# An FFT filter, a soft mixture of experts and a gated MLP in one kernel: the order of the copies in a software-pipelined loop, and the steps in which its side work is issued

## The chip, the cores and the metric

One core of one Trainium2 chip. The metric is the device time in microseconds, median of the runs; the kernel before took 1748.12 us (three runs, 1746.44 to 1748.21).

## The reference

Eight sequences of 3072 tokens and 256 channels (`x`) go through three layers, all in float32:

1. a frequency filter: `X = rfft(x)` along the sequence, a complex 256 x 256 product with `w_r + i w_i` and a bias, a soft threshold of 0.01 on the real and imaginary part, and `irfft`;
2. a soft mixture of experts over all 24576 tokens and 32 slots: `logits = x @ phi`, a softmax over the tokens (`d`) that mixes tokens into slots, eight small two-layer experts on four slots each, and a softmax over the slots (`c`) that spreads the slots back to tokens;
3. a gated MLP: RMS norm, `silu(xn @ w_gate) * (xn @ w_val)`, times `w_out`; its weights come as 64-bit floats.

```python
X = rfft(x); Y = soft(X.real @ w_r - X.imag @ w_i + b_r) + 1j * soft(X.real @ w_i + X.imag @ w_r + b_i)
x = irfft(Y).reshape(-1, 256)
logits = x @ phi;  d = softmax(logits, axis=0);  slot_in = d.T @ x
c = softmax(logits, axis=1);  x = c @ experts(slot_in)
xn = x / rms(x) * rms_g;  out = (silu(xn @ w_gate) * (xn @ w_val)) @ w_out
```

## The kernel before

Two phases. **Phase 2** (from about 655 us on) is the gated MLP; the change leaves it alone. **Phase 1** takes the eight sequences ("batches" below) through the filter and gathers the slots. The result of the filter is never transformed back for all tokens; logits and slot sums are formed from the frequencies.

Phase 1 is one loop of 288 **steps**: 36 per batch, in three windows of 12 (`w`, `m = u % 12`). Each step issues for TensorE, in this order: a part of **M** (the complex product, `emit_M`, one or three matmuls, in the two `psM` banks), then where they fall on the step: `emit_0`, **A** (first stage of the transform of the next batch, eight groups a batch, `emit_A`, in `psC`), **T** (turning the filtered frequencies, `emit_T`, in `psT` or `psA`), **L** (products with `phi`, `emit_L`, same banks), **B** (second stage of the next window, `emit_B`, in two `psB` banks), and last the parts of the **slots' chain** of the batch before that belong to TensorE. All engines work their queues in program order.

Work that follows a matmul is not issued with it but put off with `post(f, k, rank)`: `f` is issued `k` steps later, at the start of that step, sorted by `rank`; after it come the chain's parts for the other engines, then the matmuls. What is put off:

- A: `asb`, a copy of `psC` to SBUF on ScalarE (L246), then two stores to a `bounce` buffer in DRAM (SyncE's queue), one step later, rank 1; the load of the input for the group three later is put off too (rank 1, ahead of it).
- B: two copies on ScalarE one step later (L282, L283), a sum and a difference on VectorE two steps later (L286, L287), rank 0.
- M: for each `psM` bank either a copy on ScalarE (L322), or `whole`, a sum on VectorE that frees the bank (L329), then `first` on ScalarE (L332) and `end` on VectorE (L335), which completes the filtered frequencies; all rank 0.
- T: a copy on ScalarE (L383); L: a turn on VectorE (L396); both one step later, rank 1.

`psC` is a single tile of two banks, used in turn by A and by the parts of the chain. `load_B` brings the bounced data of the next batch back (four transfers on SyncE's queue, L260); its first quarter for a new batch is issued at step 23, and TensorE needs it at step 27.

**The chain** (`chain(b)`, a list of step, function and a mark for TensorE's parts): `binv`, `t1`, `ainv` (logits by token, two matmuls into `psC`, each copied by ScalarE, L437), `dmax` (L448, the largest logit of each slot over the batch), `dpar` (a reduction across partitions on GpSimd, L453, `PARTITION_ALL_REDUCE`), `dmn`, `dsub` (VectorE), `dexp` (ScalarE); beside it `cmax`, `csub` (GpSimd, L497), `cexp`, `csum`, `cmul` (GpSimd, L511) and a store of `c` to DRAM (L513, SyncE); then `fa`, `t2` (VectorE, L528), `fb`, `dT`, `slot`, `s_up`.

**The converter** (`converter`, 18 pieces) makes float32 of the MLP's weights: a load (L128), six to eight VectorE operations (L144 to L155), a product on GpSimd (L156) and a store (L165); the last six pieces also a ScalarE copy (L160) and a difference on GpSimd (L162). It is a generator; the loop takes its next step (to the next `yield`) when a running sum `load` of VectorE work, kept from the hand-written tables `fixed` and `chained` and the number `pace`, is under `room`.

Ahead of the loop the first batch's eight A groups run straight through: 16 loads on SyncE's queue, then two stores to `bounce` a group, with the loads of `bf`, `wf` and `w_i` behind the fifth group's stores, then `load_B(0, 0)`, on which TensorE's first B waits.

Of the kernel before, what the change touches and what calls it, by code (L numbers as in the profile page):

```python
# [6 lines left out]
F32 = mybir.dt.float32  # L7
# [3 lines left out]
ALU = mybir.AluOpType  # L11
# [98 lines left out]
def converter(tc, st, w_gate, w_val, w_out, wgv_d, wo_d):  # L110

    nc = tc.nc
    raw_p, tmp_p = pool(tc, st, "cvr", 2), pool(tc, st, "cv", 1)
    jobs = []
    for i, w in enumerate((w_gate, w_val)):
        v = w.bitcast(I32).rearrange("(k p) f -> p k f", p=128)
        for k in range(2):
            for f in range(3):
                jobs.append((v[:, k, 1024 * f:1024 * f + 1024], wgv_d[:, k, 1536 * i + 512 * f:1536 * i + 512 * f + 512]))
    v = w_out.bitcast(I32).rearrange("(k p) c -> p k c", p=128)  # L120
    for k in range(0, 12, 2):
        jobs.append((v[:, k:k + 2, :], tuple(w[:, k:k + 2, :].rearrange("p k c -> p (k c)") for w in wo_d)))

    def load(n):
        t = raw_p.tile([128, 512, 2], I32, name="cvraw")
        v = jobs[n][0]
        d = t.rearrange("p n w -> p (n w)")
        nc.sync.dma_start(out=d if len(v.shape) == 2 else d.rearrange("p (k f) -> p k f", k=2), in_=v)  # L128
        return t

    def steps():
        v = nc.vector
        nxt = load(0)
        yield
        for n, (_, dst) in enumerate(jobs):
            t = nxt
            if n + 1 < len(jobs):
                nxt = load(n + 1)
            lo, hi = t[:, :, 0], t[:, :, 1]
            p = tmp_p.tile([128, 512], I32, name="cva")  # L140
            m = tmp_p.tile([128, 512], I32, name="cve")
            q = tmp_p.tile([128, 512], I32, name="cvr")

            v.tensor_scalar(out=p, in0=hi, scalar1=0x7FF00000, scalar2=None, op0=ALU.bitwise_and)  # L144
            v.tensor_scalar(out=p, in0=p, scalar1=float(896 << 20), scalar2=float(1151 << 20), op0=ALU.max, op1=ALU.min)
            yield
            v.tensor_scalar(out=p, in0=p, scalar1=float(896 << 20), scalar2=8.0, op0=ALU.subtract, op1=ALU.mult)
            v.scalar_tensor_tensor(out=p, in0=hi, scalar=-(1 << 31), in1=p, op0=ALU.bitwise_and, op1=ALU.bitwise_or)
            yield
            v.tensor_scalar(out=m, in0=hi, scalar1=3, scalar2=0x7FFFFF, op0=ALU.logical_shift_left, op1=ALU.bitwise_and)  # L150
            v.tensor_scalar(out=m, in0=m, scalar1=0x3F800000, scalar2=None, op0=ALU.bitwise_or)
            yield
            v.tensor_scalar(out=q, in0=lo, scalar1=8, scalar2=0xFFFFFF, op0=ALU.logical_shift_right, op1=ALU.bitwise_and)
            w = m.bitcast(F32)
            v.scalar_tensor_tensor(out=w, in0=q, scalar=2.0 ** -44, in1=w, op0=ALU.mult, op1=ALU.add)  # L155
            nc.gpsimd.tensor_tensor(out=w, in0=w, in1=p.bitcast(F32), op=ALU.mult)  # L156
            if isinstance(dst, tuple):
                h = q.bitcast(F32)
                yield
                nc.scalar.activation(out=h.bitcast(F32R), in_=w, func=AF.Copy)  # L160
                nc.sync.dma_start(out=dst[0], in_=h)
                nc.gpsimd.tensor_tensor(out=w, in0=w, in1=h, op=ALU.subtract)  # L162
                nc.sync.dma_start(out=dst[1], in_=w)
            else:
                nc.sync.dma_start(out=dst, in_=w)  # L165
            yield
    return steps()


def phase1(tc, x, w_r, w_i, b_r, b_i, phi, t_d, t_bf, t_ci, t_ai, t_af, t_id,  # L170
# [56 lines left out]
    def emit_A(g, banks=None):  # L227
# [16 lines left out]
        def evac():  # L244
# [6 lines left out]
            for h in range(2):  # L251
                f = 512 * (2 * i + h)
                nc.sync.dma_start(out=v[:, :, f:f + 512], in_=Y[64 * h:64 * h + 48].rearrange("k (o f) -> k o f", o=2))
        post(evac)

    def load_B(b, q):
        t = bin_p.tile([128, 4, 256], F32, name="bin")
# [39 lines left out]
    def emit_M(b, qq, m):  # L297
# [36 lines left out]
        def end():  # L334
            nc.vector.scalar_tensor_tensor(out=Y, in0=Y, scalar=b_hi[:, ri, ch:ch + 1], in1=r[:, o:], op0=ALU.add, op1=ALU.min)  # L335
            if m == 11:
                xq.pop((b, qq))
                xs.pop((b, qq))
        post(whole, 1 + late, 0)
        post(first, 2 + late, 0)  # L340
        post(end, 3 + late, 0)

# [30 lines left out]
    def emit_T(b, q, ri, ps=None):  # L373
        Y = yy[b, q // 2]
        if (b, q) not in yts:
            yts[b, q] = new_yt(b, q)
        ps = new_t() if ps is None else ps
        for par in range(2):
            for h in range(2):
                o = 256 * par + 128 * h  # L380
                nc.tensor.transpose(out=ps[:, o:o + 128], in_=ysl(Y, slice(q % 2, q % 2 + 1), h, ri, par), identity=ident)
        yt = yts[b, q]
        post(lambda: nc.scalar.activation(out=yt[:, 2 * ri:2 * ri + 2, :].rearrange("p a c -> p (a c)"), in_=ps, func=AF.Copy))  # L383

    def emit_L(b, qq):
        Y = yy[b, qq]
# [6 lines left out]
                nc.tensor.matmul(out=ps[32 * g:32 * g + 32, 0:256], lhsT=ph[:, h, :],  # L393
                                 rhs=ysl(Y, slice(0, 2), h, ri, par), start=(h == 0), stop=(h == 1))
        lf = lfs[b]
        post(lambda: nc.vector.transpose(out=lf[:, 8 * qq:8 * qq + 8, :].rearrange("p a s -> p (a s)"), in_=ps[:, 0:256]))  # L396

    def bank(p, n):
        return p.tile([128, 512], F32, name=n)
# [4 lines left out]
    def chain(b):  # L404
# [20 lines left out]
        def ainv(k, own=None):  # L425
            if k == 0:
                S["l"] = ch_p.tile([128, 1024], F32, name="ch")[0:96]
            s = slice(512 * k, 512 * k + 512)
            if own:
                ps = S["l", 16 * k] = bank(*own)[0:96]  # L430
            else:
                if k == 0:
                    S["ps"] = new_c()
                ps = S["ps"][0:96, s]
            nc.tensor.matmul(out=ps, lhsT=ai, rhs=S["t1"][:, s], start=True, stop=True)
            if not own:
                post(lambda: nc.scalar.activation(out=S["l"][:, s], in_=ps, func=AF.Copy))  # L437

        def lcopy(k):
            nc.scalar.activation(out=S["l"][:, 512 * k:512 * k + 512], in_=S["l", 16 * k], func=AF.Copy)  # L440
# [65 lines left out]
            nc.vector.tensor_scalar(out=sc, in0=sc, scalar1=1e-9, scalar2=None, op0=ALU.add)  # L506
            nc.vector.reciprocal(out=sc, in_=sc)

        def cmul():
            S["c"] = ch_p.tile([128, 1024], F32, name="ch")[0:96]  # L510
            nc.gpsimd.tensor_tensor(out=S["c"].rearrange("p (n s) -> p n s", s=32), in0=S["e"].rearrange("p (n s) -> p n s", s=32),  # L511
                                    in1=S["sc"].unsqueeze(2).to_broadcast([96, 32, 32]), op=ALU.mult)
            nc.sync.dma_start(out=c_d[b], in_=S["c"])  # L513

# [9 lines left out]
        def t2(s0, s1):  # L524
            if s0 == 0:
                S["t2"] = ch_p.tile([128, 1024], F32, name="ch")
            ps = S["ps"][:, 32 * s0:32 * s1] if s1 - s0 == 32 else S["ps", s0]
            nc.vector.transpose(out=S["t2"].rearrange("p (a s) -> p s a", s=32)[:, s0:s1],  # L528
                                in_=ps.rearrange("p (s n) -> p s n", n=32))

# [63 lines left out]
            return lambda: f(*a)  # L594

        if b < NB - 1:
            return [(5, clear), (6, L(binv, 0, 24), 1), (7, L(t1, 0, 32)), (8, L(ainv, 0), 1), (9, L(ainv, 1), 1),
                    (12, L(dmax, 0, 32)), (13, L(dpar, 32)), (14, cmax), (15, csub), (18, L(dmn, 32)), (18, L(dsub, 0, 32)),
                    (19, L(dexp, 0, 32)), (19, alexp), (20, cexp), (21, csum), (22, cmul), (22, L(fa, 0, 16), 1),
                    (23, L(fa, 16, 32), 1), (24, L(t2, 0, 32)), (25, alT),  # L600
                    (26, L(fb, 0, 12), 1), (27, L(fb, 12, 24), 1), (29, L(dT, 0, 6)),
                    (31, lambda: slot(0, 6, new_c()), 1), (33, s_up)]

        def tr(q, ri, k):
            return lambda: emit_T(b, q, ri, bank(*((psT, "psT"), (psM, "psM"), (psM, "psM"), (psA, "psA"), (psB, "psB"))[k]))
# [47 lines left out]
    banks = [(psA, "psA"), (psT, "psT"), (psB, "psB"), (psB, "psB"), (psM, "psM"), (psM, "psM")]  # L653
    for g in range(8):
        emit_A(g, [bank(*banks[2 * (g % 3) + o]) for o in range(2)])
        if g == 4:
            load_bf(0, nc.sync)
            for t, w in ((wf, w_r), (rw[:, 0:512].rearrange("p (k m) -> p k m", k=2), w_i)):
                nc.sync.dma_start(out=t, in_=w.rearrange("(k p) m -> p k m", p=128))
    warm_up(14)  # L660
    prep_w()
    load_B(0, 0)
# [7 lines left out]
    for c in range(-6, 0):  # L670
# [9 lines left out]
            emit_A(8)  # L680
        elif c == -2:
            emit_B(0, 1, 1)
    first = [1, 4, 6, 9, 11, 14, 17] + [36 * b + u for b in range(NB - 2) for u in (34, 36, 38, 47, 49, 51, 53, 55)]
    first = {u: 9 + g for g, u in enumerate(first)}


# [4 lines left out]


    fixed = (1.8, 0.75, 0.75, 0.0, 0.0, 1.55, 0.7, 1.1, 1.45, 0.0, 1.85, 0.7)
    chained = {5: 0.3, 7: 1.1, 12: 1.8, 14: 1.2, 18: 1.5, 21: 1.6, 24: 2.0, 29: 1.0, 30: 2.0, 33: 0.5, 34: 2.0}
    load, room, pace = 0.0, 1.0, 1.72
    for u in range(S):
        w, m = divmod(u, 12)
        b, qq = divmod(w, 3)
# [492 lines left out]
```

## Time and profile before

| | |
|---|---|
| median of three runs | 1748.12 us |
| the profiled execution, whole | 1743.32 us |
| its span, first to last instruction | 1741.5 us |
| TensorE busy | 1679.0 us (96%) |
| VectorE busy | 1289.5 us (74%) |
| ScalarE busy | 1026.0 us (59%) |
| GpSimd busy | 106.6 us (6%) |
| mean granted TensorE clock | 0.993 |

The page is one execution. TensorE is busy nearly throughout, so the time is its work plus the time in which it waits; the rows that matter are those that tell what it waited for, and in which stage. A matmul's end is modelled, so its busy time runs a little past the start of the next.

### The profile page before, as it was taken

What the parts mean: (1) busy time and instruction counts of PE and PEld (TensorE: products, weight loads), DVE (VectorE), ACT (ScalarE), POOL (GpSimd) and SP (SyncE); (2) the same over time, 40 slices, a digit from 0 to 9 for tenths busy, and PEclk for the clock granted to TensorE, in tenths of its full rate; (3) what the DMA queues carried; (4) which work ended last, traced back from release to release, by engine and by line L of the source; (5) the groups of instructions that cost most, each with busy time, mean ns of one, the idle gap of its engine ahead of it and who ended that gap; (6) DMA issues with size and microseconds to landing.
All of it is one profiled execution on the core that took longest, in us unless ns stands there. A gap on an engine that the chain in (4) does not pass through costs nothing.

```text
span 1741.5 us, 27023 instructions
## 1 busy us (share of the span) xinstructions
PE 1679.0 (96%) x10173; PEld 1289.7 (74%) x10173; DVE 1289.5 (74%) x2257; ACT 1026.0 (59%) x1942; POOL 106.6 (6%) x74
## 2 busy tenths in 40 slices
PE   6999998989999899999999999999999999999999
PEld 3565554645556547888888888888888888888887
DVE  3577776676665758877877887887887887787775
ACT  2555545445554437666666666666666666666664
POOL 0001201020220101000000000000000000000000
PEclk8999999999999999999999999999999999999999
DMA  9875665556556483020021021021021020020001
GB/s 245 253 211 158 201 159 165 148 157 186 136 152 203 141 262 99 25 63 29 17 61 34 25 61 34 25 61 34 25 61 34 25 60 25 22 60 26 25 25 37
DMA packets 111138, 164.20 MB, mean 94 GB/s; under 512 B 15376, under 2 KB 76528, under 8 KB 111008
## 3 DMA queue, kind: packets, MB, share of 16 engines
q1 hardware_dynamic: 107456, 161.66, 32.0%
q8 instruction: 80, 1.31, 0.3%
q10 hardware_dynamic: 3376, 0.62, 0.2%
q0 software_dynamic: 176, 0.20, 0.1%
q14 instruction: 50, 0.41, 0.1%
HBM read 90.08 MB, written 59.77 MB: 86 GB/s over the span
## 4 chain that ended last, share of the span: by engine, by line
PE 83%; DVE 6%; ACT 5%; DMA 4%; issue 1%; SPq 1%; POOL 0%; ACTq 0%; DVEq 0%; POOLq 0%
PE po L1092 15%; PE pe L1092 15%; PE po L1093 8%; PE pe L1093 8%; PE pg L1064 8%; PE pv L1066 8%; PE psM L316 5%; PE psB L273 4%; PE psC L240 3%; PE psM L311 2%; ACT asb L246 1%; DMA bounce<-asb 1%; PE psC L576 1%; DVE yy L329 1%; DVE yy L335 1%
## 5 line engine op out<-in xcount | busy, mean ns | idle before, releaser
L1070 DVE TENSOR_TENSOR h<-s,pv 128x512 f32<-128x512 f32 x576 | 395.2, 686 | 189.2 <-ACT s L1068 180.5
L1068 ACT ACTIVATE s<-pg 128x512 f32<-128x512 f32 x576 | 344.7, 599 | 300.4 <-PE pg L1064 298.9
L1092 PE MATMUL po<-wo,hh 128*128 128x512 f32 x1152 | 429.2, 396 | 0.0
L1092 PE MATMUL pe<-wo,hh 128*128 128x512 f32 x1152 | 425.6, 394 | 0.0
L107 DVE TENSOR_TENSOR hl<-h,hh 128x512 fp32r<-128x512 f32 x572 | 400.4, 700 | 0.1
L106 ACT ACTIVATE hh<-h 128x512 fp32r<-128x512 f32 x576 | 359.7, 625 | 1.0 <-DVE h L1070 0.9
L1093 PE MATMUL po<-wo,hl 128*128 128x256 f32 x1152 | 323.9, 281 | 0.0
L1093 PE MATMUL pe<-wo,hl 128*128 128x256 f32 x1152 | 322.8, 280 | 0.0
L1092 PEld LDWEIGHTS po<-wo,hh 128*128 128x128 f32 x1152 | 216.8, 188 | 50.9
L1092 PEld LDWEIGHTS pe<-wo,hh 128*128 128x128 f32 x1152 | 216.5, 188 | 49.4
L1093 PEld LDWEIGHTS pe<-wo,hl 128*128 128x128 f32 x1152 | 216.5, 188 | 22.7
L1064 PE MATMUL pg<-cq,gst 128*128 128x512 f32 x576 | 228.7, 397 | 0.3 <-ACT s L1068 0.3
L1066 PE MATMUL pv<-cq,gst 128*128 128x512 f32 x576 | 226.3, 393 | 1.0 <-DVE h L1070 1.0
L1093 PEld LDWEIGHTS po<-wo,hl 128*128 128x128 f32 x1152 | 216.2, 188 | 2.7
L316 PE MATMUL psM<-xq,wh 128*128 128x512 f32 x384 | 165.8, 450 | 6.0 <-DVE yy L329 5.2
L282 ACT ACTIVATE xq<-psB 128x512 fp32r<-128x512 f32 x96 | 57.2, 596 | 144.0 <-PE psB L273 143.8
L1064 PEld LDWEIGHTS pg<-cq,gst 128*128 128x128 f32 x576 | 108.4, 188 | 26.8 <-ACT s L1068 1.1
L332 ACT ACTIVATE r<-yy,b_lo 128x512 f32<-128x512 f32 (+1 forms) x92 | 66.9, 727 | 92.4 <-DVE yy L329 46.6
L273 PEld LDWEIGHTS psB<-bf,bin 128*128 128x128 f32 x768 | 98.1, 197 | 30.6 <-issue 27.2
L273 PE MATMUL psB<-bf,bin 128*128 128x128 f32 x768 | 105.3, 282 | 15.1 <-DMA bin<-bounce 15.1
L286 DVE TENSOR_TENSOR xs<-psB,xs 128x256 f32<-128x256 f32 x96 | 40.5, 421 | 102.6 <-ACT xs L283 102.6
L1066 PEld LDWEIGHTS pv<-cq,gst 128*128 128x128 f32 x576 | 108.8, 189 | 2.3 <-DVE h L1070 2.2
(229 smaller groups left out, 1762.1 us busy)
## 6 DMA issues: line engine op xcount, KB each, us to landing
bin<-bounce SPq DMA_DIRECT2D x192, 128.0 KB, 3.8
out_dram<-o SPq DMA_DIRECT2D x47, 512.0 KB, 2.9
xraw<-in_x_dram SPq DMA_DIRECT2D x112, 192.0 KB, 4.0
bounce<-asb SPq DMA_DIRECT2D x112, 192.0 KB, 3.6
ex<-in_moe_w_dram SPq DMA_DIRECT2D x16, 1024.0 KB, 9.5
cq<-chi SPq DMA_DIRECT2D x56, 96.0 KB, 2.1
cq<-clo SPq DMA_DIRECT2D x56, 96.0 KB, 2.1
yt<-in_x_dram SPq DMA_DIRECT2D x16, 192.0 KB, 6.1
```

The source lines that it names most:

```text
L106: nc.scalar.activation(out=hi, in_=src, func=AF.Copy)
L107: (lo_eng or nc.vector).tensor_tensor(out=lo, in0=src, in1=hi.bitcast(F32), op=ALU.subtract)
L273: nc.tensor.matmul(out=ps[:, 128 * j:128 * j + 128], lhsT=t[:, j, 128 * h:128 * h + 128], rhs=bf[:, 4 * q + j, :], start=True, stop=True)
L282: nc.scalar.activation(out=hi, in_=v, func=AF.Copy)
L316: nc.tensor.matmul(out=ps, lhsT=w[k - 1][:, h, cs], rhs=X[:, p, h, k - 1], start=(h == 0 and n == 0), stop=(h == 1 and n == 2))
L332: nc.scalar.activation(out=r[:, o:], in_=Y, func=AF.Relu, bias=b_lo[:, ri, ch:ch + 1])
L1064: nc.tensor.matmul(out=pg, lhsT=gst[:, 128 * fb:128 * fb + 128], rhs=v, start=True, stop=True)
L1066: nc.tensor.matmul(out=pv, lhsT=gst[:, 1536 + 128 * fb:1536 + 128 * fb + 128], rhs=v, start=True, stop=True)
L1068: nc.scalar.activation(out=s, in_=pg, func=AF.Silu)
L1070: nc.vector.tensor_tensor(out=h, in0=s, in1=pv, op=ALU.mult)
L1092: nc.tensor.matmul(out=ps, lhsT=hh[:, ts], rhs=wo[:, fb].rearrange("p k c -> p (k c)"), start=(fb == 0), stop=False)
L1093: nc.tensor.matmul(out=ps[:, 0:256], lhsT=hl[:, ts], rhs=wo[:, fb, 0], start=False, stop=(fb == 11))
```

## The change

The copies and sums that free a PSUM bank or feed TensorE next (`asb`, `whole`, the copies of T, of `ainv`, the turn of L) get rank -1: they come first in their step on their engine. The second `ainv` writes to a `psT` or `psA` bank and no longer to the second half of `psC`. The converter's product and difference go from GpSimd to VectorE, each after a `yield` of its own; `csub` of the chain goes from GpSimd to VectorE. `dsub` and `t2` are split into halves. The parts of the chain, the A groups (`first`), T, L and B are put on other steps; L from step 4 to 6 of a window, the fourth B from 10 to 9. The tables that pace the converter change with it. Ahead of the loop, the loads of `bf`, `wf` and `w_i` are issued behind all eight groups' stores.

```diff
@@ converter
-            nc.gpsimd.tensor_tensor(out=w, in0=w, in1=p.bitcast(F32), op=ALU.mult)
+            yield
+            v.tensor_tensor(out=w, in0=w, in1=p.bitcast(F32), op=ALU.mult)
...
-                nc.gpsimd.tensor_tensor(out=w, in0=w, in1=h, op=ALU.subtract)
+                yield
+                v.tensor_tensor(out=w, in0=w, in1=h, op=ALU.subtract)
@@ emit_A
-        post(evac)
+        post(evac, 1, -1)
@@ emit_M
-        post(whole, 1 + late, 0)
+        post(whole, 1 + late, -1)
@@ emit_T, emit_L (their copy and turn)
-        post(lambda: ...)
+        post(lambda: ..., 1, -1)
@@ chain
-            if own:
-                ps = S["l", 16 * k] = bank(*own)[0:96]
+            if own or k:
+                ps = S["l", 16 * k] = (bank(*own) if own else new_t())[0:96]
...
-                post(lambda: nc.scalar.activation(out=S["l"][:, s], in_=ps, func=AF.Copy))
+                post(lambda: nc.scalar.activation(out=S["l"][:, s], in_=ps, func=AF.Copy), 1, -1)
...
-            return [(5, clear), (6, L(binv, 0, 24), 1), (7, L(t1, 0, 32)), (8, L(ainv, 0), 1), (9, L(ainv, 1), 1),
-                    (12, L(dmax, 0, 32)), (13, L(dpar, 32)), (14, cmax), (15, csub), (18, L(dmn, 32)), (18, L(dsub, 0, 32)),
-                    (19, L(dexp, 0, 32)), (19, alexp), (20, cexp), (21, csum), (22, cmul), (22, L(fa, 0, 16), 1),
-                    (23, L(fa, 16, 32), 1), (24, L(t2, 0, 32)), (25, alT),
-                    (26, L(fb, 0, 12), 1), (27, L(fb, 12, 24), 1), (29, L(dT, 0, 6)),
-                    (31, lambda: slot(0, 6, new_c()), 1), (33, s_up)]
+            return [(5, clear), (7, L(binv, 0, 24), 1), (8, L(t1, 0, 32)), (9, L(ainv, 0), 1), (10, L(ainv, 1), 1),
+                    (12, L(dmax, 0, 32)), (12, L(dpar, 32)), (11, cmax), (14, L(csub, nc.vector)), (13, L(dmn, 32)),
+                    (15, L(dsub, 0, 16)), (17, L(dsub, 16, 32)),
+                    (19, L(dexp, 0, 32)), (16, alexp), (17, cexp), (21, csum), (23, L(cmul, nc.gpsimd)), (20, L(fa, 0, 16), 1),
+                    (21, L(fa, 16, 32), 1), (22, L(t2, 0, 16)), (23, L(t2, 16, 32)), (25, alT),
+                    (25, L(fb, 0, 12), 1), (25, L(fb, 12, 24), 1), (26, L(dT, 0, 6)),
+                    (30, lambda: slot(0, 6, new_c()), 1), (32, s_up)]
@@ phase1, ahead of the loop
-        if g == 4:
-            load_bf(0, nc.sync)
-            for t, w in ((wf, w_r), (rw[:, 0:512]..., w_i)):
-                nc.sync.dma_start(out=t, in_=...)
+    load_bf(0, nc.sync)
+    for t, w in ((wf, w_r), (rw[:, 0:512]..., w_i)):
+        nc.sync.dma_start(out=t, in_=...)
@@ phase1, the loop
-    first = [1, 4, 6, 9, 11, 14, 17] + [36 * b + u for b in range(NB - 2) for u in (34, 36, 38, 47, 49, 51, 53, 55)]
+    first = [3, 4, 6, 9, 11, 15, 16] + [36 * b + u for b in range(NB - 2) for u in (33, 37, 40, 46, 47, 48, 52, 55)]
...
-    chained = {5: 0.3, 7: 1.1, 12: 1.8, 14: 1.2, 18: 1.5, 21: 1.6, 24: 2.0, 29: 1.0, 30: 2.0, 33: 0.5, 34: 2.0}
-    load, room, pace = 0.0, 1.0, 1.72
+    chained = {7: 1.1, 12: 1.9, 13: 1.2, 17: 2.2, 20: 1.7, 22: 2.0, 28: 1.0, 34: 0.5}
+    load, room, pace = 0.0, 0.4, 1.8
...
-        if w >= 1 and m in (2, 5, 8, 10) and w <= W - 3:      # T
+        if w >= 1 and m in (2, 4, 7, 11) and w <= W - 3:
-        if w >= 1 and m == 4:                                  # L
+        if w >= 1 and m == 6:
-        if w + 1 < W and m in (3, 5, 8, 10):                   # B
+        if w + 1 < W and m in (3, 5, 8, 9):
```

## Rows read from the trace of the kernel before

**Rows 1.** Busy time by stretch (us, instructions), granted clock, DMA share, GB/s.
```profile
40.00:97.00 57.00, 54.98 (x331) 34.58 (x331) 32.51 (x64) 31.89 (x59) 1.28 (x1) 1.00 0.92 257
473.00:604.00 131.00, 122.92 (x951) 77.21 (x949) 87.70 (x148) 66.64 (x124) 15.98 (x10) 1.00 0.52 161
```
**Rows 2.** The same view for five batches, the first of them and their sum.
```profile
97.00:169.00 72.00, 68.15 (x514) 41.61 (x513) 53.36 (x95) 37.90 (x70) 9.68 (x6) 1.00 0.62 173
...
sum 376.30, PE 345.59 PEld 210.75 DVE 268.60 ACT 191.42 POOL 53.59; mean PE 69.12 PEld 42.15 DVE 53.72 ACT 38.28 POOL 10.72
```
**Rows 3.** TensorE's waits, 40 to 604 us: waiter, releaser, total us, times, longest.
```profile
PE psC L240 <- ACT asb L246: 11.6, 19, 5.4
PE psM L311 <- DVE yy L329: 7.2, 6, 2.0
PE psM L316 <- DVE yy L329: 5.2, 3, 2.3
PE psC L435 <- ACT ch L437: 5.0, 7, 1.0
PE psB L273 <- DMA bin<-bounce: 4.0, 2, 2.4
PE psT L381 <- DVE yy L335: 2.9, 3, 1.0
PE psA L381 <- DVE yy L335: 2.6, 3, 0.9
```
**Rows 4.** Timeline 344 to 361 us: start, us, engine, line, operation, idle time before.
```profile
346.55 0.84 POOL L453 PARTITION_ALL_REDUCE mb<-mx  x1 [18.96 <-DVE mx L448]
...
350.11 0.69 DVE L155 SCALAR_TENSOR_TENSOR cve<-cvr,cve 128x512 f32<-128x512 int32 x1
...
355.31 1.25 POOL L156 TENSOR_TENSOR cve<-cve,cva 128x512 f32<-128x512 f32 x1 [7.92 <-DMA bounce<-asb]
...
356.60 0.63 ACT L160 ACTIVATE cvr<-cve 128x512 fp32r<-128x512 f32 x1 [6.88 <-POOL cve L156]
...
359.44 1.99 PE L240 MATMUL psC<-xraw,dt 48*64 48x512 f32 x8 [5.38 <-ACT asb L246]
```
**Rows 5.** Timeline 143 to 151 us, where batch 1's third window begins.
```profile
145.21 0.69 DVE L329 TENSOR_TENSOR yy<-psM,s 128x512 f32<-128x512 f32 x1
...
145.95 2.84 PE L311 MATMUL psM<-xs,wf 128*128 128x512 f32 x6 [1.21 <-DVE yy L329]
...
147.34 1.91 DVE L528 STREAM_TRANSPOSE ch<-psC 128x1024 f32<-128x1024 f32 x1
...
148.63 0.27 PE L381 MATMUL psA<-ident,yy 128*128 128x128 f32 x1
...
149.84 0.55 PE L381 MATMUL psA<-ident,yy 128*128 128x128 f32 x3 [0.94 <-DVE yy L335]
```
**Rows 6.** Timeline 215 to 227 us, SyncE's queue and TensorE's first B.
```profile
216.32 0.31 SPq L513 DMA_DIRECT2D c_d<-ch  x1
...
216.73 0.38 SPq L128 DMA_DIRECT2D cvraw<-in_moe_w_val_dram  x1
...
225.57 1.13 PE L273 MATMUL psB<-bf,bin 128*128 128x128 f32 x8 [1.60 <-DMA bin<-bounce]
```
**Rows 7.** Timeline 606 to 611 us: `dmn` of the last batch.
```profile
609.51 0.26 DVE L463 TENSOR_REDUCE mn<-mb 128x32 f32<-128x96 f32 x1 [0.72 <-POOL mb L453]
```
**Rows 8.** Line 497 where it runs on VectorE: ns shortest/median/longest, when.
```profile
L497 DVE TENSOR_TENSOR ch<-ch,mc x1: 1223/1223/1223, 623.9 to 623.9; 96x1024 f32<-96x1024 f32 x1
```
**Rows 9.** VectorE's waits, 97 to 473 us, columns as in rows 3.
```profile
DVE xs L286 <- ACT xs L283: 60.2, 38, 3.5
DVE cva L144 <- POOL cve L156: 15.8, 5, 7.4
```
**Rows 10.** Timeline 18 to 33 us, ahead of the loop.
```profile
18.59 0.67 SPq L651 DMA_DIRECT2D bf<-in_t_bf_dram  x1
...
32.54 0.77 PE L273 MATMUL psB<-bf,bin 128*128 128x128 f32 x2 [11.07 <-DMA bin<-bounce]
```

More of the change, by code (lines that the diff above doesn't have):

```diff
@@ L382, in emit_T @@
         yt = yts[b, q]
-        post(lambda: nc.scalar.activation(out=yt[:, 2 * ri:2 * ri + 2, :].rearrange("p a c -> p (a c)"), in_=ps, func=AF.Copy))
+        post(lambda: nc.scalar.activation(out=yt[:, 2 * ri:2 * ri + 2, :].rearrange("p a c -> p (a c)"), in_=ps, func=AF.Copy), 1, -1)
     def emit_L(b, qq):
@@ L395, in emit_L @@
         lf = lfs[b]
-        post(lambda: nc.vector.transpose(out=lf[:, 8 * qq:8 * qq + 8, :].rearrange("p a s -> p (a s)"), in_=ps[:, 0:256]))
+        post(lambda: nc.vector.transpose(out=lf[:, 8 * qq:8 * qq + 8, :].rearrange("p a s -> p (a s)"), in_=ps[:, 0:256]), 1, -1)
     def bank(p, n):
@@ L428, in ainv @@
             s = slice(512 * k, 512 * k + 512)
-            if own:
-                ps = S["l", 16 * k] = bank(*own)[0:96]
-            else:
-                if k == 0:
-                    S["ps"] = new_c()
+            if own or k:
+                ps = S["l", 16 * k] = (bank(*own) if own else new_t())[0:96]
+            else:
+                S["ps"] = new_c()
                 ps = S["ps"][0:96, s]
@@ L507, in csum, with cmul @@
             nc.vector.reciprocal(out=sc, in_=sc)
-        def cmul():
+        def cmul(eng=nc.gpsimd):
             S["c"] = ch_p.tile([128, 1024], F32, name="ch")[0:96]
-            nc.gpsimd.tensor_tensor(out=S["c"].rearrange("p (n s) -> p n s", s=32), in0=S["e"].rearrange("p (n s) -> p n s", s=32),
+            eng.tensor_tensor(out=S["c"].rearrange("p (n s) -> p n s", s=32), in0=S["e"].rearrange("p (n s) -> p n s", s=32),
                                     in1=S["sc"].unsqueeze(2).to_broadcast([96, 32, 32]), op=ALU.mult)
@@ L526, in t2 @@
                 S["t2"] = ch_p.tile([128, 1024], F32, name="ch")
-            ps = S["ps"][:, 32 * s0:32 * s1] if s1 - s0 == 32 else S["ps", s0]
+            ps = S["ps"][:, 32 * s0:32 * s1] if b < NB - 1 else S["ps", s0]
             nc.vector.transpose(out=S["t2"].rearrange("p (a s) -> p s a", s=32)[:, s0:s1],
@@ L655, in phase1 @@
         emit_A(g, [bank(*banks[2 * (g % 3) + o]) for o in range(2)])
-        if g == 4:
-            load_bf(0, nc.sync)
-            for t, w in ((wf, w_r), (rw[:, 0:512].rearrange("p (k m) -> p k m", k=2), w_i)):
-                nc.sync.dma_start(out=t, in_=w.rearrange("(k p) m -> p k m", p=128))
+    load_bf(0, nc.sync)
+    for t, w in ((wf, w_r), (rw[:, 0:512].rearrange("p (k m) -> p k m", k=2), w_i)):
+        nc.sync.dma_start(out=t, in_=w.rearrange("(k p) m -> p k m", p=128))
     warm_up(14)
@@ L727, in phase1 @@
             emit_A(first[u])
-        if w >= 1 and m in (2, 5, 8, 10) and w <= W - 3:
-            k = (2, 5, 8, 10).index(m)
+        if w >= 1 and m in (2, 4, 7, 11) and w <= W - 3:
+            k = (2, 4, 7, 11).index(m)
             emit_T(*divmod(2 * (w - 1) + k % 2, 6), 1 - k // 2)
-        if w >= 1 and m == 4:
+        if w >= 1 and m == 6:
             emit_L(*divmod(w - 1, 3))
-        if w + 1 < W and m in (3, 5, 8, 10):
-            k = (3, 5, 8, 10).index(m)
+        if w + 1 < W and m in (3, 5, 8, 9):
+            k = (3, 5, 8, 9).index(m)
             emit_B(*divmod(2 * (w + 1) + k // 2, 6), k % 2)
@@ L740, in phase1 @@
         load = max(0.0, load + fixed[(u + 1) % 12] + chained.get((u + 1) % 36, 0.0) - pace)
-        if load < room and (u == 12 or u > 14):
+        if load < room and (u == 12 or u > 12 + 2):
             next(conv, None)
```

## The prediction

> **What bounds the kernel now.** I read the page's busy shares first: TensorE is busy 96% of the span, so the change can only win what TensorE waits. Next the busy time by stretch, to see where it waits; then the list of its waits, to see for whom; then the timeline at the longest of each kind.
>
> Phase 2 is left alone and TensorE is full there, so everything lies ahead of 604 us. Five full batches take 376.3 us, in which TensorE is busy 345.6: 30.7 us idle [rows 2]. Their busy time should be the same, yet the mean is 69.1 us against 68.15 in the first, the one at full clock; the 4.8 us above 5 x 68.15 are matmuls at a lower granted clock behind long waits [rows 2]. The stretches on either side add 57.0 - 55.0 and 131.0 - 122.9, 10.1 us [rows 1]. Lastly, a wait is counted from a modelled end that lies behind the next start when nothing waits: the six matmuls from 145.95 end at 148.79 by the row, and the next starts at 148.63 [rows 5]. That hides 0.16 us of each wait; the groups shown hold 43 waits [rows 3], 6.9 us. So 30.7 + 4.8 + 10.1 + 6.9 = **52.5 us** lie in waits of the loop. ScalarE and VectorE are not full: VectorE is busy 268.6 of 376.3 us, 71% [rows 2]; TensorE waits for the place of a copy in its queue, not for the engine's capacity.
>
> **The change, part by part.** Each kind of wait, what becomes of it, and what is late next. Durations are of the profiled execution (1743.3 us whole); the sum is taken from it and carried over to the median, 1748.1, as a difference.
>
> *GpSimd as a link.* In batch 4 the reduction across partitions starts at 346.55 and is recorded with 0.84 us, but the next GpSimd instruction, a converter product whose input was ready at 350.8, starts only at 355.31; ScalarE's converter copy sits idle 6.88 us for it, with `asb` queued behind, and TensorE waits 5.38 us for `asb` [rows 4]. Batch 3 has the same chain through VectorE, which waits up to 7.4 us for the converter product [rows 9], and TensorE up to 2.3 us for VectorE's `whole` behind that [rows 3]. With the converter's two operations and `csub` on VectorE, nothing but `cmul` is left behind the reduction, eleven steps later. These waits go. Price: 18 products and 6 differences at 0.69 us, the duration of a like operation [rows 4], 16.6 us, and seven `csub` at 1.22 [rows 8], 8.5 us: 25.1 us more on VectorE over seven batches, about 3.6 a batch beside some 21.5 idle. I cost that at nothing, and at 9.3 us net if its cover is gone (the rival of VectorE). The Trainium skill's page GPSIMD Engine Reference, section Instruction dispatch, says that the first call of freshly loaded code pays about 6 us that no instruction shows; the 7.92 us idle behind the reduction are of that kind [rows 4], and where the load stood ahead of the reduction, the sum would be that of the late reduction below.
>
> *M at a window's start, T behind it.* At 145.95 M waits for `whole`, which stood behind a converter operation and B's difference; then `t2` takes 1.91 us of VectorE from 147.34, `end` is late behind it, and T waits until 149.84 [rows 5]. These are 7.2 us in 6 waits and 5.5 us in 6 [rows 3]. The change puts `whole` first in its step and `t2` in halves into the two steps ahead, before `whole` and the last B sum. By program order VectorE then has only `whole` to do at step 24 and `end` at 25. What is next late: `fb`, both halves now at step 25, needs the second half of `t2`; I put 0.4 us a batch there, and 0.2 at step 0, where a converter operation may still stand ahead of `whole`.
>
> *The second `ainv`* waits for the copy of the first half of `psC` in every batch, 5.0 us in 7 [rows 3]. In a bank of its own it needs no copy: gone.
>
> *A waits for `asb`*: 11.6 us in 19 waits, 6.2 in 18 without the one of batch 4, 0.34 each [rows 3]. With rank -1 `asb` no longer stands behind B's two copies. But three A groups now follow each other in steps 10 to 12, and the first of them needs `psC` freed by a copy of `ainv` in its own step. I leave two waits of 0.34 a batch in six batches. Bounds: none, and up to 5.4, the longest such wait, if the third `asb` must wait for the stores of the first (two buffers) with the DMA engines crowded; the nearest row is the short one, since in three steps TensorE does more work than one copy takes.
>
> *The first B of a new batch*: its load stands on SyncE's queue behind the store of `c`, which waits for `cmul`. At 216.32 the store goes, a converter load slips in at 216.73, and B starts at 225.57 after waiting [rows 6]; two batches lose 4.0 us so [rows 3]. Worked through step by step, the new tables give the converter no step from 16 to 24 of a batch, so nothing slips in. Against it, B comes some 2 us sooner after the last A, because parts of the chain leave those steps, while the store hangs on `csum`, which stays at 21. I count that as even: the two waits gone, none new; at worst both stay.
>
> *Ahead of the loop*: the stores of groups 6 to 8 move ahead of three loads, whose issue takes about three times 0.67 us [rows 10]. TensorE waits 11.07 us for the first B there [rows 10]. Between 0 and 2.0 us; I take 1.0, since the same bytes still go through before `load_B` has landed.
>
> *Cheap parts.* L two steps later: the turn comes first in its step and `binv` moves along; the fourth B a step earlier: its bank was freed three steps before. `new_t` is called once more per batch and shifts the order of the two banks only. `dmn` at step 13 waits for the reduction issued in step 12: where VectorE had nothing else to do, it was released 0.72 us after `dmax` ended [rows 7], and `end` goes ahead of it. Nothing.
>
> Sum: what stays is 6 x 2 x 0.34 + 7 x (0.4 + 0.2) = 8.3 us. 52.5 - 8.3 + 1.0 = 45.2 us off: the profiled execution at 1698, the median at 1748.1 - 45.2 = **1703 us**.
>
> **The rivals.**
>
> *The regular waits stay.* The waits for `asb`, `whole`, `ainv`'s copy and `end` return at other steps, since a copy that comes first still waits for its own producer. They are 6.2 + 7.2 + 5.0 + 5.5 = 23.9 us, and 37 x 0.16 more, 29.8. The gain is 52.5 - 29.8 + 1.0 = 23.7, the time 1724 us. For it: rank changes no producer. Against: at 145.21 `whole` starts long after its matmuls, behind other VectorE work [rows 5]. This holds too the case that the change doesn't do what it says.
>
> *No change at all* would need new waits of 45 us, 6.5 a batch, from several of these together: 1748.
>
> *VectorE becomes the bound (slower).* If its idle time is no reserve but waiting for B's copies in order (60.2 us for L283 [rows 9]), it can't take more work. Then the 25.1 us add to the loop, less the 15.8 us that it waited for GpSimd [rows 9]: 9.3 us more and nothing won, 1757 us. It decides once VectorE's waits don't shrink as work comes in. Against: those waits are ended by TensorE's own matmuls through ScalarE, so VectorE was early. The Trainium skill's page Perfetto Trace Analysis, section Optimizing Scalar/DVE Operations, says that moving work off a saturated VectorE can pay and that between GpSimd and VectorE it might not help; read backwards it speaks against loading VectorE. At 71% it is not saturated here.
>
> *The reduction comes late.* If its result were there only when GpSimd goes on, 8.8 us after its start [rows 4], `dmn` at step 13 would hold VectorE for 8 us a batch. Half of it reaching TensorE, 7 x 4 = 28, gives 1731 us; all of it, 1759. Against: the 0.72 us [rows 7].
>
> **How the numbers follow.** Forecast 0.60, regular waits stay 0.18, reduction late 0.10, VectorE bound 0.07, no change 0.05. The predicted time is the forecast's, 1703 us. Low end: all 52.5 and 2.0 ahead of the loop, 1694, and a microsecond for the runs' spread, 1693. High end 1731, which takes in the regular waits and half the late reduction; beyond it lie the bound VectorE, no change, and the rest of the late reduction. About 0.2% is what a measurement of this kernel can tell from none. Faster by more: 0.60 + 0.18 + most of the late reduction, 0.86; within: 0.05; slower: 0.09.
>
> **What would show it.** In the profile after: the waits of TensorE for L246, L329, L335 and L437's lines shrink to under a quarter, a batch takes 68 to 69 us with VectorE busy near 57, GpSimd shows only the reduction and `cmul`, and no low clock appears in the loop. Wrong would be: a wait of M or L behind `dmn`, TensorE waiting for B's load in most batches, A waiting long in steps 10 to 16, or a batch still over 71 us.

## The result and the profile after

| | before | after |
|---|---|---|
| median | 1748.16 us (4 runs, 1746.44 to 1752.62) | 1692.34 us (4 runs, 1690.05 to 1694.29) |
| the profiled execution, whole | 1743.32 us | 1694.29 us |
| ratio after / before | | 0.9676, 95% interval 0.9652 to 0.9701 |

55.8 us off, 3.2%. The forecast was 1703 (1693 to 1731): the direction was right, the gain was 10.6 us larger, and the time lies 0.7 us under the low end.

After the change most lines stand one or two further down: A is L242, its copy `asb` L248, B L275, M L313 and L318, `whole` L331, `end` L337, T L383, its copy L385, the reduction L454, `csub` L498. The page of the kernel after, busy time and the chain of work that ended last:

```profile
PE 1670.2 (99%) x10173; PEld 1294.2 (76%) x10173; DVE 1299.4 (77%) x2302; ACT 1036.2 (61%) x1942; POOL 55.8 (3%) x43
...
PE 95%; DVE 2%; DMA 1%; ACT 1%; SPq 0%; issue 0%; ACTq 0%; POOL 0%; DVEq 0%; POOLq 0%
```

TensorE is busy 99% of the span. Busy time by stretch, kernel after, columns as in [rows 1]; the second and third are batches 1 and 2:

```profile
40.00:97.00 57.00, 55.94 (x341) 35.37 (x338) 34.95 (x68) 34.28 (x61) 0.00 (x0) 1.00 0.88 254
97.00:163.60 66.60, 66.60 (x515) 42.12 (x514) 54.81 (x102) 39.43 (x68) 3.00 (x2) 1.00 0.67 186
163.60:230.20 66.60, 66.53 (x515) 42.08 (x514) 55.43 (x104) 39.43 (x69) 2.86 (x2) 1.00 0.69 184
```

Batch 1 took 72.0 us [rows 2] and takes 66.6, and batches 1 to 5 now last 66.6 us each; before they took 72 to 80. TensorE is busy practically throughout them. All of its larger waits from 35 to 560 us, kernel after, columns as in [rows 3]:

```profile
PE psA L395 <- ACT yt L385: 1.2, 1, 1.2
PE psM L318 <- ACT s L324: 0.8, 1, 0.8
PE psC L418 <- DVE lf L398: 0.6, 1, 0.6
PE psM L313 <- DVE xs L288: 0.6, 1, 0.6
PE psM L313 <- DVE yy L331: 0.5, 1, 0.5
PE psA L383 <- DVE yy L337: 0.5, 1, 0.5
```

The first and the third come at 552 and 553 us, behind the loop that is defined below. Of [rows 3], the 11.6 us for `asb`, the 5.0 for `ainv`'s copy and the 4.0 for B's load are gone; of 12.4 for `whole` 0.5 is left, of 5.5 for `end` 0.5.

A second measure is used below. The **loop** is the time from M's first matmul to the first one of M's last window (276 of 288 steps). First and last row of it, kernel before:

```profile
40.04 1.02 PE L311 MATMUL psM<-xs,wf 128*128 128x512 f32 x2
...
584.08 2.74 PE L311 MATMUL psM<-xs,wf 128*128 128x512 f32 x6
```

and kernel after:

```profile
41.15 1.02 PE L313 MATMUL psM<-xs,wf 128*128 128x512 f32 x2
...
532.88 1.98 PE L313 MATMUL psM<-xs,wf 128*128 128x512 f32 x4 [0.54 <-DVE yy L331]
```

That is 544.0 against 491.7 us: 52.3 off. Busy time in these two stretches, before and after, columns as in [rows 1]:

```profile
40.04:584.08 544.04, 504.05 (x3635) 311.28 (x3634) 376.56 (x668) 282.92 (x519) 70.85 (x45) 0.99 0.61 172
41.15:532.88 491.73, 489.00 (x3635) 311.81 (x3633) 386.98 (x712) 292.83 (x518) 20.17 (x14) 1.00 0.68 190
```

TensorE's idle time in the loop fell from 40.0 to 2.7 us, and its busy time, for the same matmuls, by 15.0 us.

### The profile page after: what moved, and what is told of

Its sections match the earlier page's. It is cut to its first block, busy times and chain, and to the rows that moved or that the text cites. A ratio compares the mean times of both kernels' runs of the same rounds, so it can differ in the third digit from the quotient of the medians.

```text
span 1692.5 us, 26967 instructions
## 1 busy us (share of the span) xinstructions
PE 1670.2 (99%) x10173; PEld 1294.2 (76%) x10173; DVE 1299.4 (77%) x2302; ACT 1036.2 (61%) x1942; POOL 55.8 (3%) x43
## 4 chain that ended last, share of the span: by engine, by line
PE 95%; DVE 2%; DMA 1%; ACT 1%; SPq 0%; issue 0%; ACTq 0%; POOL 0%; DVEq 0%; POOLq 0%
PE po L1093 16%; PE pe L1093 16%; PE po L1094 8%; PE pe L1094 8%; PE pg L1065 8%; PE pv L1067 8%; PE psM L318 7%; PE psB L275 5%; PE psM L313 5%; PE psC L242 3%; PE psT L383 1%; PE psC L577 1%; PE psA L383 1%; PE psA L395 1%; PE psC L418 1%; PE psC L545 1%
## 5 line engine op out<-in xcount | busy, mean ns | idle before, releaser
L318 PE MATMUL psM<-xq,wh 128*128 128x512 f32 x384 | 171.6, 457 | 0.8 <-ACT s L324 0.8
L275 PEld LDWEIGHTS psB<-bf,bin 128*128 128x128 f32 x768 | 101.3, 194 | 32.4 <-issue 10.3
L275 PE MATMUL psB<-bf,bin 128*128 128x128 f32 x768 | 103.9, 279 | 8.1 <-DMA bin<-bounce 8.1
L313 PE MATMUL psM<-xs,wf 128*128 128x512 f32 x192 | 96.6, 609 | 1.1 <-DVE xs L288 0.6
L318 PEld LDWEIGHTS psM<-xq,wh 128*128 128x128 f32 x384 | 72.5, 189 | 30.7 <-issue 20.0
```

Source lines behind the costliest of these rows:

```text
L275: nc.tensor.matmul(out=ps[:, 128 * j:128 * j + 128], lhsT=t[:, j, 128 * h:128 * h + 128], rhs=bf[:, 4 * q + j, :], start=True, stop=True)
L313: nc.tensor.matmul(out=ps, lhsT=wf[:, h, cs], rhs=xs[b, qq][:, h], start=(h == 0), stop=(h == 1))
L318: nc.tensor.matmul(out=ps, lhsT=w[k - 1][:, h, cs], rhs=X[:, p, h, k - 1], start=(h == 0 and n == 0), stop=(h == 1 and n == 2))
```

## Experiments

Runs without a median are one profiled execution; their loop is compared with 491.4, the mean of two executions of after (491.7 and 491.0).

**How far one execution stands for the kernel.** Four more executions, of unchanged kernels.

> The kernel before once more, for a second trace. If the executions of before differ by which long stalls they have, the loop's 544.1 us (first M to the last window's first M) will differ by some us and the waits for B's load or behind GpSimd with it; if by the clock at the phases' border only, the loop is 544 again.

> The kernel before, a third trace. Theory: an execution's time is a constant of some 1200 us plus its loop, and the loop varies with the number of stretches at the lower clock behind TensorE's waits (four such stretches ahead of 604 us and 544.0 in the first trace, seven and 553.7 in the second): so time minus loop is 1199 to 1202 here too, and the loop lies between 542 and 555. Rival: the loop is 544 and the spread lies in phase 2.

> A fourth trace of the kernel before, for the same: time minus loop 1199 to 1202, the loop between 542 and 555 with the number of stretches at the lower clock.

> The changed kernel once more, beside the kernel before on one chip. If the difference of the two profiled executions (1743.3 - 1694.3 = 49.0 us) is the change's own and the rest of the median's 55.8 us is spread between executions, the ratio lies near 0.972; if the medians tell the change's own part, it is 0.968 again, and the kernel before must hold something that its one profiled execution doesn't show.

| | whole | loop | whole less loop | TensorE idle in the loop | of the loop at half clock |
|---|---|---|---|---|---|
| before | 1743.32 | 544.0 | 1199.3 | 40.0 | 13.7 |
| before again | 1753.98 | 553.7 | 1200.2 | 43.8 | 23.9 |
| before, third | 1747.88 | 544.3 | 1203.5 | 40.2 | 13.7 |
| before, fourth | 1746.36 | 546.7 | 1199.7 | 40.2 | 17.1 |
| after | 1694.29 | 491.7 | 1202.6 | 2.7 | none |
| after again | 1688.85 | 491.0 | 1197.8 | 2.3 | none |

After again had a median of 1693.77 us, ratio 0.9686 (0.966 to 0.9713). The four loops of before have a mean of 547.2 us and the two of after 491.4: 55.8 off, the difference of the medians. What is outside the loop didn't change (means 1200.7 and 1200.2), though it varies by some 4 to 5 us between executions of either kernel. The execution on which the forecast rests had the shortest loop of four, 3.2 us under their mean. The third has almost the same loop, and what it takes longer lies outside it (1203.5, above the 1199 to 1202 that were expected). Where the same kernel's loop is longer, there are longer waits in it or more time at half clock. One place in the second execution of before, columns as in [rows 1]:

```profile
74.00:77.00 3.00, 0.67 (x3) 0.58 (x4) 3.00 (x7) 0.96 (x2) 0.00 (x0) 1.00 0.95 287
77.00:81.00 4.00, 4.00 (x19) 3.54 (x18) 2.79 (x6) 2.18 (x5) 0.00 (x0) 0.57 0.51 159
```

and in the first:

```profile
74.00:77.00 3.00, 3.00 (x20) 2.64 (x21) 2.15 (x5) 1.52 (x3) 0.00 (x0) 1.00 0.92 252
77.00:81.00 4.00, 3.48 (x20) 2.45 (x19) 3.96 (x9) 3.05 (x7) 0.00 (x0) 1.00 0.43 130
```

Where TensorE stood idle (busy 0.67 of 3 us), the next stretch was granted 0.57 of the clock, 1.2 instead of 2.4 GHz for most of it; where it didn't, the clock stayed at 1.00. The longest wait in the loop of the kernel after is 0.85 us, and its loop repeats to 0.7 us.

**GpSimd as a link.** The three operations go back to GpSimd in the kernel after, together, and then in two parts (`csub` alone; the converter's two alone):

```diff
-            v.tensor_tensor(out=w, in0=w, in1=p.bitcast(F32), op=ALU.mult)
+            nc.gpsimd.tensor_tensor(out=w, in0=w, in1=p.bitcast(F32), op=ALU.mult)
-                v.tensor_tensor(out=w, in0=w, in1=h, op=ALU.subtract)
+                nc.gpsimd.tensor_tensor(out=w, in0=w, in1=h, op=ALU.subtract)
-  (14, L(csub, nc.vector))
+  (14, csub)
```

> The changed kernel with the converter's product and difference and csub back on GpSimd, the yields kept. The prediction's link: what is queued behind the reduction starts some 8 us late. csub is at step 14 and cexp at 17, so ScalarE should stand still for about 8 + 2 - 6 = 4 us in each of seven batches, and the converter's steps on VectorE behind it: 25 to 50 us back, 1717 to 1742. If GpSimd cost only the two long stalls of the kernel before, it is 11.5 us: about 1704.

> The changed kernel with csub alone back on GpSimd. All three operations back cost 28 us. If the cost is the 8 us behind the reduction, csub, which is the next GpSimd instruction in each of seven batches and which ScalarE's cexp and then VectorE's csum wait for, carries most of it: 15 to 22 us, 1708 to 1715. If the converter's 24 operations carry it, under 5 us: below 1698.

> The changed kernel with the converter's product and difference alone back on GpSimd. By the same theory only those products that fall behind a reduction cost (two to four of eighteen): 4 to 12 us, 1697 to 1705. If GpSimd is merely the slower engine (1.28 against 0.69 us for each), nothing comes back, since the converter has no due time: 1693.

| | median | ratio to before (95%) | loop | loop against after |
|---|---|---|---|---|
| all three back | 1720.43 | 0.9847 (0.9819 to 0.9875) | 519.0 | +27.6 |
| `csub` alone | 1708.77 | 0.9781 (0.9766 to 0.9797) | 507.5 | +16.1 |
| the converter's alone | 1699.34 | 0.9723 (0.9708 to 0.9739) | 499.7 | +8.3 |

Timeline of the kernel with all three back, 118 to 138 us:

```profile
118.48 1.22 DVE L494 TENSOR_REDUCE mc<-ch 96x32 f32<-96x1024 f32 x1 [1.03 <-ACT ch L438]
...
122.28 0.84 POOL L454 PARTITION_ALL_REDUCE mb<-mx  x1 [21.46 <-DVE mx L449]
...
123.16 0.18 DVE L468 COPY mn<-mb 128x32 f32<-128x32 f32 x1 [0.35 <-POOL mb L454]
...
130.60 1.91 POOL L498 TENSOR_TENSOR ch<-ch,mc 96x1024 f32<-96x1024 f32 x1 [7.49 <-issue]
...
132.49 1.27 POOL L157 TENSOR_TENSOR cve<-cve,cva 128x512 f32<-128x512 f32 x1
...
132.55 1.06 ACT L502 ACTIVATE ch<-ch 96x1024 f32<-96x1024 f32 x1 [3.15 <-POOL ch L498]
...
133.79 0.43 DVE L144 TENSOR_SCALAR cva<-cvraw 128x512 int32<-128x512 int32 x1 [8.27 <-POOL cve L157]
...
137.10 0.80 PE L318 MATMUL psM<-xq,wh 128*128 128x512 f32 x1 [2.92 <-DVE yy L331]
```

The reduction is recorded with 0.84 us and its result is there at once (`dmn`, L468, starts 0.04 us behind its end), but GpSimd starts its next instruction 7.49 us behind it, and 7.2 to 9.2 us in the other batches. That instruction, `csub`, had its inputs long before: the last of them, `mc`, was written by 119.70. Through `csub`, ScalarE's exponential waits 3.15 us, through the product VectorE's converter 8.27, and behind both of them stand copies and sums that TensorE waits for. The losses all lie in steps 17 to 21 of a batch. That `csub` itself takes 1.91 us on GpSimd and 1.22 on VectorE makes under 5 us in seven batches and so can't be the 16.1.

The same three moves alone, in the kernel before, with its old steps and ranks:

```diff
-            nc.gpsimd.tensor_tensor(out=w, in0=w, in1=p.bitcast(F32), op=ALU.mult)
+            v.tensor_tensor(out=w, in0=w, in1=p.bitcast(F32), op=ALU.mult)
...
-  (15, csub)
+  (15, L(csub, nc.vector))
```

> The kernel before with the converter's two operations and csub on VectorE, in the steps and ranks of before and without new yields. The prediction put the long stalls on this link: 11.5 us in the trace of before and part of the last batch's waits, so 1733 to 1738. If in the old steps VectorE is too late for its 25 us more, the waits for whole and end grow: 1745 or more.

Median 1730.13 us, ratio 0.9901 (0.9884 to 0.9917), 17.6 us off and 3 more than was expected at most; loop 530.6, 16.6 under the mean of before, 13.4 under its first execution. The expectation's 11.5 us is no sum that the prediction gives; the two waits that it puts on this link, 5.4 us for `asb` and 2.3 for `whole` [rows 3], make 7.7. What stayed, TensorE's waits of this kernel, 35 to 600 us:

```profile
PE psM L311 <- DVE yy L329: 7.0, 6, 1.9
PE psC L240 <- ACT asb L246: 6.6, 19, 0.5
PE psC L435 <- ACT ch L437: 4.9, 7, 0.7
PE psM L316 <- DVE yy L329: 3.9, 2, 2.5
...
PE psB L273 <- DMA bin<-bounce: 1.5, 2, 1.2
```

The 11.6 us for `asb` of [rows 3] are 6.6 without the long one, as the forecast split them (6.2). The wait of 2.3 us for `whole` in batch 3 is gone; the 3.9 us left on that line are two other waits, at 76 and 567 us. The waits for B's load fell from 4.0 to 1.5.

**Ranks or steps.** All ranks back in the kernel after; and, on top of the kernel before with GpSimd's three on VectorE, first only the ranks, then only the chain's new steps with the second `ainv` in a bank of its own:

```diff
-        post(evac, 1, -1)
+        post(evac)
-        post(whole, 1 + late, -1)
+        post(whole, 1 + late, 0)
...
```

> The changed kernel with all five ranks of -1 back at 0 and 1; the steps and engines stay. If the order within a step is what removes the regular waits (asb, whole, the copy of ainv, end: 29.8 us), most of them come back: 1692 + 20 to 30 = 1712 to 1722. If the steps on which the work lies do it, under 5 us come back: below 1697.

> The kernel before with the three operations on VectorE (its loop, first M to the last window's first M, was 530.6 us) and the five ranks of -1 besides. The prediction held the copy's place in its step to be what A waits for: 6.6 us in 19 waits and 0.16 hidden in each should go, and part of the 7.0 us for whole: the loop at 515 to 521. If ranks do nothing in the old steps either, as they did nothing in the new ones, 529 to 531.

> The same kernel with the new steps of the slots' chain (halves of dsub and t2, second ainv in a bank of its own) in place of the ranks; A, T, L, B and the converter's tables stay as before. If the chain's steps cure the waits at a window's start, behind t2 and for the copy of ainv: 7.0 + 4.7 + 4.9 us and 19 x 0.16, the loop falls to some 511. If VectorE's order around them needs the converter's new tables, under half of it goes: above 520.

All ranks back in after: 1692.37 us, ratio 0.9684 (0.9661 to 0.9706), the time of after; loop 493.8, +2.4. Batches 1 to 6 agree step by step. In batch 0 three waits for `asb` come back:

```profile
PE psC L242 <- ACT asb L248: 2.8, 3, 1.2
```

The ranks alone took the loop from 530.6 to 517.6 us (1720.72 whole), the chain alone to 519.4 (1719.44 whole), which lies between the two cases of its expectation. Waits with the ranks:

```profile
PE psM L311 <- DVE yy L329: 5.9, 6, 1.3
PE psM L316 <- DVE yy L329: 2.8, 2, 2.0
PE psA L381 <- DVE yy L335: 2.7, 3, 0.9
PE psT L381 <- DVE yy L335: 2.3, 3, 0.9
...
PE psC L240 <- ACT asb L246: 0.5, 2, 0.2
```

and with the chain's steps:

```profile
PE psC L240 <- ACT asb L246: 9.6, 19, 0.7
PE psM L316 <- DVE yy L329: 3.1, 1, 3.1
PE psA L381 <- DVE yy L335: 2.3, 6, 0.4
...
PE psM L311 <- DVE yy L329: 1.0, 2, 0.8
```

Each cures other waits: the ranks all but end A's (6.6 to 0.5) and leave most of the window's start (7.0 to 5.9); the chain's steps end most of the window's start (7.0 to 1.0) and leave A's, which even grow (6.6 to 9.6). The wait for `ainv`'s copy is gone from both lists. With the other parts in place the ranks change nothing from batch 1 on. The likely reason is that the new steps already keep apart what the ranks put first; no run shows that by itself.

**Places of T, L, B and A.** In the kernel after, T, L and B back on the old steps; the fourth B alone; the A groups alone:

```diff
-        if w >= 1 and m in (2, 4, 7, 11) and w <= W - 3:
+        if w >= 1 and m in (2, 5, 8, 10) and w <= W - 3:
-        if w >= 1 and m == 6:
+        if w >= 1 and m == 4:
-        if w + 1 < W and m in (3, 5, 8, 9):
+        if w + 1 < W and m in (3, 5, 8, 10):
```

> The changed kernel (loop 491.0 to 491.7) with T, L and B back on their old steps of a window. If they were moved for nothing that TensorE waits for, the loop stays below 493. If the last B's sum at step 12, in front of dmax and end, makes T at step 14 late again and the fourth B wait, 5 to 10 us come back: 496 to 501.

> The changed kernel with the fourth B alone back from step 9 to 10 of a window. With T, L and B back the loop was 500.7 and M waited for B's sums. If the fourth B is the whole of that, 498 to 501; if the places of T and L carry it, below 494.

> The changed kernel with the A groups back on their old steps. If A's waits for asb hang on how many B copies stand between two groups and the next, they return in part although asb comes first: 6.6 us in 18 waits, the loop at 495 to 500. If rank -1 is what cured them, nothing returns: below 493.

T, L and B back: 1702.07 us, loop 500.7, +9.3; the batches have 67.7 to 67.9 us instead of 66.6. M now waits for B's sum, in small waits:

```profile
PE psM L313 <- DVE xs L288: 5.9, 16, 1.3
```

The fourth B alone costs 1.1 us (loop 492.5, 1695.56 whole). T and L without it weren't run, so whether the other 8.2 are theirs, or come from the three together, is open. The A groups on their old steps cost nothing (loop 491.4, 1693.93 whole), with `asb` at rank -1.

**Ahead of the loop.** The three loads back behind the fifth group:

```diff
+        if g == 4:
+            load_bf(0, nc.sync)
...
-    load_bf(0, nc.sync)
```

> The changed kernel with the loads of bf, wf and w_i back behind the fifth group's stores. The prediction gave this part 1.0 us of gain: by it this run is 1 us slower than the changed kernel, about 1693.3. By the trace after, where the loop starts at 41.2 us instead of 40.0, the part costs 1.2 us: by that this run is 1.2 us faster, about 1691.

1692.12 us, ratio 0.9684 (0.966 to 0.9709), after's time. The first B, in this kernel:

```profile
32.79 3.75 PE L275 MATMUL psB<-bf,bin 128*128 128x128 f32 x16 [10.98 <-DMA bin<-bounce]
```

and in two executions of after:

```profile
32.81 3.75 PE L275 MATMUL psB<-bf,bin 128*128 128x128 f32 x16 [8.11 <-DMA bin<-bounce]
```

```profile
31.88 3.63 PE L275 MATMUL psB<-bf,bin 128*128 128x128 f32 x16 [11.72 <-DMA bin<-bounce]
```

Two executions of one kernel differ by more than the two heads; neither expectation shows. Executions with the old head enter the loop between 40.0 and 43.8 us, those with the new one between 39.4 and 43.4, so a microsecond either way can't be seen here.

## Why the prediction was right, and where it failed

| | forecast | first execution of each | mean of 4 before, of 2 after |
|---|---|---|---|
| loop | -52.5 + 8.3 = -44.2 | -52.3 | -55.8 |
| ahead of it | -1.0 | +1.1 | |
| behind it | 0 | +2.2 | outside the loop together: -0.5 |
| whole | -45.2 | -49.0 | -56.3 (medians: -55.8) |

- **What bounds it: right, and nearly to the size.** The waits of the loop were summed to 52.5 us; 52.3 went. That what A waited for was the place of a copy in its queue is shown by the run with the ranks alone, where the same work on the same engines took these waits from 6.6 to 0.5 us. The two corrections that the list of waits doesn't show, 6.9 us behind modelled ends and 4.8 us of low clock, were needed: TensorE's busy time fell by 15.0 us, and they foresaw 11.7 of it. That the sums agree to 0.2 us is in part luck, since 2.7 us of idle time stayed and 0.8 of the 40.8 that were counted lie behind the loop.
- **The 8.3 us that stay: the first term that failed.** Neither A's two waits of 0.34 a batch nor `fb`'s 0.4 nor the 0.2 at step 0 shows in the list after; for M at a window's start it has 0.5 us, once. So a batch takes 66.6 us and not the 68 to 69 that were to show it. The run with old steps for A has no wait for `asb` either, so with `asb` first in its step A's places, which that term priced, decide nothing.
- **One execution carried over to the median: the second.** The difference was worked out from 1743.32 us and put on 1748.1 unchanged. But that execution's loop was the shortest of four, and on the mean of the four (1747.9 whole, loop 547.2) 3.2 of the 4.6 us above it are loop, waits and low clock that go as well. 52.5 + 3.2 = 55.7 off the median gives 1692.4; measured 1692.3. It agrees so closely by chance, since the four loops lie 9.7 us apart and one execution's excess lies outside the loop. The two terms, 8.3 + 3.2, less the 1.0 us ahead of the loop that wasn't seen, make 10.5 of the 10.6 us that the forecast was off. The low end, 1693, let nothing stay but was built on the shortest loop's 52.5 us, and so fell 0.7 us short.
- **GpSimd's link: right in kind, too small.** The prediction put 7.7 us of listed waits on it. Moving the three operations took 17.6 us off the median in the old steps; moving them back costs 27.6 us of loop in the new ones, where `csub` stands two steps behind the reduction. What came along stood in other terms of the sum, so the total held: the waits for B's load (4.0 to 1.5 us), and the low clock, 13.7 us of the loop in the first execution of before, 10.2 of them behind the two waits on this link, and 3.4 in the kernel with the three moved.
- **The price on VectorE: nothing, right.** The moved operations take 24.8 us there (12.2 + 4.1 + 8.5; 25.1 forecast). VectorE's records in sum, over the whole program, rose only by 16.4 us, mainly since in the kernel before eight of its instructions stood 10.0 us longer in sum than the median of their lines, beside GpSimd's operations (shown at the end). VectorE is busy 54.8 of batch 1's 66.6 us, 82%, not near 57, and nobody waits for it for long. The bound VectorE fell as a rival.
- **The late reduction fell**: `dmn` starts 0.04 us behind the reduction's end, and VectorE stood idle for it for 0.35 us (0.72 in [rows 7]).
- **The regular waits stay: fell.** Neither part did it alone: the ranks left 5.9 us at the window's start and 5.0 at T, the chain 9.6 for `asb`. With all the new places the ranks can go for 2.4 us, all of it in batch 0.
- **L and the fourth B at nothing: wrong in the new set.** T, L and B on the old steps together cost 9.3 us there, the fourth B alone 1.1. The forecast asked what moving them would add, and not what their old place would cost once the rest had moved.
- **Ahead of the loop: 1.0 forecast, none to be seen** in a spread of some 4 us.
- **The first B of a batch: right.** Both waits of [rows 3] went and none came.

The parts don't add up to the whole. In the kernel before, moving GpSimd's three gave 16.6 us of loop, and on top of that the ranks alone 13.0 or the chain alone 11.2. Taken out of the kernel after, GpSimd's part costs 27.6, the ranks 2.4, the places of T, L and B 9.3. Not run by themselves are the converter's new tables and `yield`s, the chain's old steps in the kernel after, and the halves of `dsub` and `t2` without the second `ainv`'s own bank; what each of these is worth is open. Open too is a small rest: batch 1 at 68.15 us busy [rows 2], less 0.16 for each of its six listed waits, comes to 67.2 against 66.6, and whether that is the order of the matmuls or hidden waits wasn't separated. No version beat the kernel after: those without a cost agree with it within the spread of its executions, and TensorE has 2.7 us of idle time left in the loop.

## What to carry to other kernels

If the engine that sets the time has only waits to lose, sum them with what hides behind modelled ends and with the low clock that follows them, and let some of them stay only where a named producer is late. Then set the profiled execution beside the median: a stage full of waits can differ from one execution to the next, here by up to 9.7 us, with its waits and the low clock behind them. Look at what an in-order queue waits for behind a reduction on a slow engine, and not at that engine's busy share: 51 us of work moved off a GpSimd that was busy 6% of the span gave 17 to 28 us. Parts of such a change can stand in for each other, so undoing one of them at the end doesn't tell what it was worth.

## What the runs showed of the hardware

**GpSimd's operations lengthen VectorE's.** Timeline of the kernel before, 356 to 360 us and 371 to 375 us:

```profile
356.54 1.90 POOL L497 TENSOR_TENSOR ch<-ch,mc 96x1024 f32<-96x1024 f32 x1
...
356.60 3.35 DVE L144 TENSOR_SCALAR cva<-cvraw 128x512 int32<-128x512 int32 x1 [5.80 <-POOL cve L156]
...
358.40 1.26 POOL L162 TENSOR_TENSOR cve<-cve,cvr 128x512 f32<-128x512 f32 x1
...
371.91 2.17 POOL L511 TENSOR_TENSOR ch<-ch,sc 96x1024 f32<-96x1024 f32 x1 [12.25 <-ACT yt L383]
...
372.23 0.41 DVE L286 TENSOR_TENSOR xs<-psB,xs 128x256 f32<-128x256 f32 x1
...
372.56 0.68 DVE L287 TENSOR_TENSOR xq<-psB,xq 128x512 fp32r<-128x512 f32 x1
...
373.16 1.21 DVE L147 TENSOR_SCALAR cva<-cva 128x512 int32<-128x512 int32 x1
```

and 434 to 440 us:

```profile
434.89 1.91 POOL L497 TENSOR_TENSOR ch<-ch,mc 96x1024 f32<-96x1024 f32 x1 [7.59 <-DVE mn L465]
...
434.92 3.76 DVE L480 TENSOR_TENSOR ch<-ch,mn 96x1024 f32<-96x1024 f32 x1
...
436.77 2.93 POOL L156 TENSOR_TENSOR cve<-cve,cva 128x512 f32<-128x512 f32 x1
```

L144 takes 0.43 us as a rule, and 3.35 here, until 0.29 us behind the end of GpSimd's second operation; L147, 0.42 as a rule, ends 0.29 us behind GpSimd's product. The sum and difference of B between them, with one operand in PSUM, keep their time. The Trainium skill, GPSIMD Engine Reference, section Key points, names contention with VectorE for instructions in a two-port performance mode or with two SBUF inputs; the trace agrees for `dsub` (L480, two SBUF inputs), which takes 3.76 us beside GpSimd instead of 1.99. Whether L144 and L147, with one input each, run in such a mode, no row shows. In the kernel after the longest L144 is 0.43 us.

**GpSimd stands still behind each reduction**, 7.2 to 9.2 us in the kernel with all three back, with the result long out. The Trainium skill, GPSIMD Engine Reference, section Instruction dispatch, gives about 6 us for the first call of freshly loaded code; the rows have an idle time of that kind, longer, and behind every reduction, and no run here shows the load itself. In the kernel after, `cmul` comes 13.16 us behind the reduction in batch 1, released by VectorE, and TensorE has no wait behind it.

**The clock's cost differs from one execution to the next**: 13.7 to 23.9 us of the loop at 1.2 GHz in the same kernel, each such stretch behind a wait of TensorE, the waits 1.9 to 6.0 us long. The kernel after, without such waits in its loop, repeats it to 0.7 us.
